# GpSimd's queue in source order, and single sums placed behind the last h product

## The chip, the cores and the metric

The kernel runs on one core of a Trainium2 chip. The metric is the device time of one execution in microseconds (us). Of a kernel there are several executions, and their median is given; one more view, the profile, comes from a single execution that was recorded instruction by instruction.

The engines of the core each have a queue of their own: TensorE (PE, matrix products and their weight loads), VectorE (DVE), ScalarE (ACT), GpSimd (POOL) and SyncE (SP). In this kernel GpSimd and SyncE issue transfers and compute nearly nothing.

## The reference

```python
def _attn_ref(q, k, v):                      # [8, 8, 576, 64] each, float32
    scores = scale * np.matmul(q, k.transpose(0, 1, 3, 2))
...
    mask = (rel >= 0) & (rel < 128)
    scores = np.where(mask, scores + bias[None], -1000000000.0)
...
    return np.matmul(attn, v)

def _moe_ref(x, w_gate, w_val, w_out):       # [4608, 512], [512, 1536] twice, [1536, 512]
    g = x @ w_gate
    silu = g * (1.0 / (1.0 + np.exp(-g)))
    return (silu * (x @ w_val)) @ w_out
```

Causal attention over a window of 128 positions with a linear bias per head; the heads side by side are x, 4608 tokens by 512, and x goes through a gated feed-forward. Inputs and output are float32 in DRAM; the kernel converts to fp16 as it loads.

## The kernel before, in words

**Attention.** The work is 36 units: four groups of two batches, nine tiles of 128 positions in each, of which the ninth holds the last 64 positions of both batches. A unit forms scores (products at L282 and L317), exponentials (ScalarE, L288 and L321), the multiplication by the mask and bias (L294), the product with V (L349), the division (L351, L352), and turns x for the second part.

**Loads.** For each tile (called its rank) there are three transfers on GpSimd's queue: k and q (`load_qk`, L191) into a pool of five buffers each, and V (`load_v`, L185) into one of twelve slots. `load` puts them in order for one rank. The queue of ranks 0 to 10 with the weights is written out by hand; from rank 11 on `attention()` calls `loads_to(i + 7)` after unit i. k and q have to be turned. Up to rank 10 TensorE does that (L215, L222); from rank 11 on a transposing transfer on SyncE's queue (L243) takes the buffer and writes kT (twelve slots) or qT (nine). A buffer of the pool comes free when its transposition has been done. From unit 24 on x is turned by such a transfer too (L370). The stores of the output (L447) go through SyncE as well.

**Feed-forward.** Nine blocks of 512 tokens, driven by the generator `ffn()`. Blocks 0 to 5 form gate and value plainly (L401) and give h = silu(gate) x value by L420 and L431, or, for the last four of twelve column blocks of block 5, by L428. Blocks 6 to 8 form them with seven products where eight would be plain (`gate_val_by_seven`, products at L627; VectorE's part at L663, L664, L670 and L679; the products `first` to `seventh` are named in the code). The output product of blocks 1 to 8 is done with seven products as well (`strassen`, L536, results by L540 and L551).

**Single sums.** Products with seven in place of eight need sums of their operands. They are formed on VectorE by short instructions of 128 x 512 in fp16: of h (`sums`, L489 to L492), of x (`x_sums`, the same lines) and of the gate and value weights (`gate_val_weight_sums`, L601 to L604, 24 in all, kept in memory that attention no longer needs). Most of them wait in a list, `later`, and `ffn()` takes one or two from it after each step (L725 in the plain blocks, L770 in the blocks by seven).

**The order.** Instructions of an engine run in the order of its queue. For the first tiles and the first steps the order on TensorE, VectorE and ScalarE is that of the source (`everything()`). After that a planner of the compiler's library orders them by its own estimates; from step 60 of `ffn()` on TensorE alone is held to the order of the source. GpSimd's and SyncE's queues and VectorE's and ScalarE's later part are the planner's.

Of the kernel before, what the change touches and what calls it, by code (L numbers as in the profile page):

```python
# [23 lines left out]
ET = mybir.EngineType  # L24
# [27 lines left out]
def kernel(  # L52
# [10 lines left out]
    nc = tc.nc  # L63
# [118 lines left out]
    def load_v(rank):  # L182
        va[rank] = va_all[rank % NV]
        for (p0, p1), src in source(v, rank):
            nc.gpsimd.dma_start(va[rank][p0:p1, :, 0:D], src)  # L185

    def load_qk(rank, which="kq"):
        for name in which:
            t_ = nat.tile([P, H, D], FP16, name=name + "n", tag=name + "n")
            for (p0, p1), src in source(k if name == "k" else q, rank):  # L190
                nc.gpsimd.dma_start(t_[p0:p1], src)  # L191
            (natk if name == "k" else natq)[rank] = t_

    def load(rank):
        if rank < 10:
            load_qk(rank)
            load_v(rank)
        else:
            load_v(rank)
            load_qk(rank)  # L200

    def transposed(name, rank):

# [184 lines left out]
    hT = {}  # L388
# [19 lines left out]
    acted = {}  # L408
# [14 lines left out]
    def val(n, m, pv, c0=0, c1=512):  # L423

        if n not in hT:
            hT[n] = hpool.tile([P, NMB, 512], FP16, name="hT", tag="hT")
        if (n, m) in by_silu:
            nc.vector.scalar_tensor_tensor(out=hT[n][:, m, c0:c1], in0=acted[(n, m)][0][:, c0:c1], scalar=2.0,  # L428
                                           in1=pv[:, c0:c1], op0=ALU.mult, op1=ALU.mult)
            return  # L430
        nc.vector.tensor_mul(hT[n][:, m, c0:c1], acted[(n, m)][1][:, c0:c1], pv[:, c0:c1])  # L431

    def gate_val(n, m):
        c0 = 384 if (n, m) in acted else 0
# [175 lines left out]
        s2, s3, s4 = xsum[n] = spare[3 * (n % 2):3 * (n % 2) + 3]  # L610
        return four_sums(a11, a12, a21, a22, s2, s3, s4)

    later = []

    def gate_val_by_seven(n):

        x = xT[n]
        A11, A12 = x[:, 0:HK, 0:256], x[:, HK:NKB, 0:256]
        S1, A22 = x[:, 0:HK, 256:512], x[:, HK:NKB, 256:512]
        S2, S3, S4 = xsum.pop(n)  # L620
        hT[n] = hpool.tile([P, NMB, 512], FP16, name="hT", tag="hT")
        live = {}

        def product(dst, w, c0, a, start=False):
            for i in range(2):
                for kb in range(HK):
                    nc.tensor.matmul(dst[:, i, :], w[:, kb, c0 + i * P:c0 + (i + 1) * P], a[:, kb, :],  # L627
                                     start=(start and i == 0 and kb == 0),
                                     stop=(i == 1 and kb == HK - 1), skip_group_check=True)

        def first(u):
            X, Y = (ps_a.tile([P, 2, 256], FP32, name=i, tag="a", bufs=4) for i in ("gX", "gY"))
            Z = ps_f.tile([P, 2, 256], FP32, name="gZ", tag="gv")
            live[u] = X, Y, Z
            product(X, G1, 2 * u * P, A11, True)
            nc.scalar.copy(Z, X)

        def fifth(u):
            Y = live[u][1]
            product(Y, tsum[u][0], 0, S1, True)  # L640
            p5 = epool.tile([P, 2, 256], FP32, name="p5", tag="exc", bufs=5)
            nc.scalar.copy(p5, Y)
            live[u] += (p5,)

        def second(u):
            Z = live[u][2]
            product(Z, G2, 2 * u * P, A12)
            s = supool.tile([P, 2, 256], FP16, name="s1", tag="tt")
            nc.scalar.activation(s, Z, AF.Silu)
            live[u] += (s,)  # L650

        def sixth(u):
            X = live[u][0]
            product(X, tsum[u][1], 0, S2)
            u2 = epool.tile([P, 2, 256], FP32, name="u2", tag="exc", bufs=5)
            nc.scalar.copy(u2, X)
            live[u] += (u2,)

        def third(u):
            X, Y, Z, p5, u2, s = live[u][:6]  # L660
            product(Y, V2, 2 * u * P, S4)
            v_ = supool.tile([P, 2, 256], FP16, name="v1", tag="uu")
            nc.vector.tensor_add(v_, Y, u2)  # L663
            nc.vector.tensor_mul(hT[n][:, 2 * u:2 * u + 2, 0:256], s, v_)  # L664

        def seventh(u):
            X, Y, Z, p5, u2, s = live[u]
            product(X, tsum[u][2], 0, S3)
            v_ = supool.tile([P, 2, 256], FP16, name="v2", tag="uu")
            nc.vector.tensor_add(v_, X, p5)  # L670
            live[u] += (v_,)

        def fourth(u):
            X, v_ = live[u][0], live[u][-1]
            del live[u]
            product(X, tsum[u][3], 0, A22)
            s = supool.tile([P, 2, 256], FP16, name="s2", tag="tt")
            nc.scalar.activation(s, X, AF.Silu)  # L678
            nc.vector.tensor_mul(hT[n][:, 2 * u:2 * u + 2, 256:512], s, v_)  # L679

        return {f.__name__: f for f in (first, second, third, fourth, fifth, sixth, seventh)}

    def seven_steps():
# [21 lines left out]
    def ffn():  # L705

        for n in range(NBLK):
            if n > 1:
                parts = chain(strassen(n - 1, 0), strassen(n - 1, 1))
            if n == 1:  # L710
                for j in range(PRE):
                    for _ in project(0, j, ps_f, "po", 1):
                        yield 1.0
            if n == SEVEN_FROM:
                break
            for m in range(NMB):
                for half, _ in enumerate(gate_val(n, m)):
                    yield 1.0
                    if n > 1 and 2 * m + half in AT:
                        next(parts)  # L720
                        yield 0.75
                    if n > 1:
                        for _ in range(1 + (len(later) > 3)):
                            if later:
                                later.pop(0)()  # L725
                if n == 1:
                    if m in (4, 6, 8, 10):
                        for _ in project(0, m // 2 - 2, ps_f, "po", 1):
                            yield 1.0
                    if m in (4, 6, 8):  # L730
                        weight_sums(m // 2 - 2)
                if n > 0 and m >= 9:
                    (at_once if n == 1 and m < 11 else later.extend)(sums(n, m - 9))
                if n + 1 == SEVEN_FROM:
                    if m == SILU_AT:
                        attention_ends()
                        by_silu.update((n, i) for i in range(m + 1, NMB))
                    if m in (SILU_AT + 1, SILU_AT + 2):
                        later.extend(gate_val_weight_sums(m - SILU_AT - 1))
                    if m == SILU_AT:  # L740
                        later.extend(x_sums(n + 1))
            if n > 1:
                assert next(parts, 0) == 0
        ends = [strassen(NBLK - 1, t) for t in range(2)]
        final = ()
        for n, k, name, which in seven_steps():
            if k == 0 and n > SEVEN_FROM:
                assert next(parts, 0) == 0
                parts = chain(strassen(n - 1, 0), strassen(n - 1, 1))
            if n == SEVEN_FROM and k in (1, 3, 10, 17):  # L750
                later.extend(gate_val_weight_sums(2 + (k + 4) // 7))
            yield 0.5
            if k % 3 == 1 and k < 42:
                next(parts)
                yield 0.75
            if k == 20 and n + 1 < NBLK:
                later.extend(x_sums(n + 1))
            if k == 35:
                later.extend(sums(n, 0))
            if name == "fourth" and which is not None and which[1] > 3:  # L760
                if which == (NBLK - 1, 5):
                    at_once(final)
                else:
                    later.extend(sums(which[0], which[1] - 3))
            if n == NBLK - 1 and k == 40:
                final = sums(n, 2)
                later.append(final.pop(0))
            for _ in range(2 if len(later) > 4 or k >= 39 or k < 7 else 1):
                if later:
                    later.pop(0)()  # L770
            if n == NBLK - 1 and k == 41:
                next(ends[0])
                yield 0.75
        assert next(parts, 0) == 0 and not later

        for t in (1, 0, 1, 0, 0, 0, 1, 0, 0, 1, 1, 1, 1):
            next(ends[t])
            yield 0.75
# [98 lines left out]
            nc.gpsimd.dma_start(dst[:, :, c0:c1], src[:, :, c0:c1])  # L877


    load_qk(1, "qk")  # L880
    load_qk(2, "q")
    load_v(0)
# [90 lines left out]
        held.close()  # L973

    everything()


# [28 lines left out]
```

## Time and profile before

| | us |
|---|---|
| median of 4 executions | 347.33 |
| lowest, highest | 346.94, 349.64 |
| the profiled execution | 349.64 |
| its span in the profile | 347.8 |
| TensorE busy in it | 331.7 |
| VectorE busy | 276.7 |
| ScalarE busy | 207.6 |
| GpSimd busy | 109.7 |

The span runs from the first to the last recorded instruction; the execution's own time is 1.84 us longer. A line of the waits names the engine that stood idle, the instruction that it stood at, and what ended the wait. In a timeline a line gives the start, the duration, the engine, the line of the kernel, the operation, and output <- inputs by the names of the program; a name such as kT at L601 to L604 is then the memory that the weight sum reuses. All line numbers are those of the kernel before.

### The profile page before, as it was taken

To read this page: it belongs to the slowest core of one execution; us is meant where nothing else is said; L and a number is where in the kernel's file an instruction comes from. 1 tells how busy PE (TensorE), PEld (TensorE's weight loads), DVE (VectorE), ACT (ScalarE), POOL (GpSimd) and SP (SyncE) were. 2 spreads that over 40 slices of the span, in tenths; PEclk is the share of its full clock that TensorE was granted. 3 is DMA by queue.
4 is the path that set the end of the run, shared out by engine and by line. 5 is a ranking of instruction groups with operands and counts; after the bars stand their busy time and mean duration, and the time that the engine had idled before them with its cause. 6 is when DMAs were issued, how large, how long until landed. Compare 5 with 4: busy or idle time off the path is not lost.

```text
span 347.8 us, 7788 instructions
## 1 busy us (share of the span) xinstructions
PE 331.7 (95%) x2983; PEld 219.3 (63%) x2983; DVE 276.7 (80%) x652; ACT 207.6 (60%) x412; POOL 109.7 (32%) x136
## 2 busy tenths in 40 slices
PE   7999987999999999999999999999999999999995
PEld 3584444344446655556556565566688878878884
DVE  5477884799978869988899999999855875775583
ACT  3758674465667557575575556563467666766750
POOL 8977585258537654735511000000000000000000
PEclk9999998999999999999999999999999999999999
DMA  9999999999999999999999203021101101011014
GB/s 151 171 180 174 153 160 170 106 125 144 152 149 136 183 159 140 184 133 165 138 158 183 89 21 92 15 57 52 62 0 62 62 0 63 1 62 60 2 62 122
DMA packets 160037, 37.37 MB, mean 107 GB/s; under 512 B 147328, under 2 KB 155648, under 8 KB 160000
## 3 DMA queue, kind: packets, MB, share of 16 engines
q0 software_dynamic: 118336, 18.62, 84.6%
q1 hardware_dynamic: 40976, 17.64, 28.5%
q10 hardware_dynamic: 688, 0.62, 0.6%
q8 instruction: 23, 0.38, 0.5%
q14 instruction: 14, 0.11, 0.1%
HBM read 37.91 MB, written 9.44 MB: 136 GB/s over the span
## 4 chain that ended last, share of the span: by engine, by line
PE 63%; DVE 21%; ACT 6%; DMA 5%; issue 3%; POOL 0%; SPq 0%; DVEq 0%; ACTq 0%
PE po L536 13%; PE pg L401 12%; PE pv L401 12%; PE gX L627 6%; PE av L349 3%; DMA wo_sb<-in_moe_w_out_dram 3%; DVE hT L431 3%; PE gY L627 3%; DVE uu L420 3%; PE ps L282 3%; PE p L536 2%; PE po L455 2%; ACT ex L288 2%; DVE S L489 2%; DVE hT L490 2%
## 5 line engine op out<-in xcount | busy, mean ns | idle before, releaser
L401 PE MATMUL pv<-xT,wv_sb 128*128 128x512 f16 (+2 forms) x320 | 76.5, 358 | 0.4 <-DVE hT L431 0.2
L401 PE MATMUL pg<-xT,wg_sb 128*128 128x512 f16 (+2 forms) x320 | 76.0, 359 | 0.3 <-DVE xT L377 0.2
L419 ACT ACTIVATE tt<-pg 128x512 f16<-128x512 f32 (+2 forms) x70 | 41.3, 590 | 50.5 <-PE pg L401 49.5
L288 ACT ACTIVATE ex<-ps 128x512 f16<-128x512 f32 x96 | 50.0, 606 | 12.0 <-PE ps L282 11.9
L420 DVE SCALAR_TENSOR_TENSOR uu<-tt,pg 128x512 f16<-128x512 f16 (+2 forms) x69 | 45.8, 664 | 10.5 <-ACT tt L419 10.2
L431 DVE TENSOR_TENSOR hT<-uu,pv 128x512 f16<-128x512 f16 (+2 forms) x70 | 46.5, 665 | 3.6 <-PE pv L401 1.6
L191 POOL DMA_DIRECT2D kn<-in_k_dram x39 | 33.1, 852 | 34.8 <-DMA kT<-kn 24.7
L401 PEld LDWEIGHTS <-wg_sb 128*128 128x128 f16 x320 | 28.3, 98 | 24.6 <-issue 2.7
L401 PEld LDWEIGHTS <-wv_sb 128*128 128x128 f16 x320 | 28.3, 98 | 23.7 <-issue 2.6
L536 PEld LDWEIGHTS <-hT 128*128 128x128 f16 x384 | 36.8, 98 | 10.0 <-issue 1.1
L185 POOL DMA_DIRECT2D va<-in_v_dram x40 | 34.1, 857 | 19.8 <-PE av L349 8.4
L191 POOL DMA_DIRECT2D qn<-in_q_dram x39 | 33.1, 852 | 16.4 <-DMA qT<-qn 6.6
L536 PEld LDWEIGHTS <-S 128*128 128x128 f16 x288 | 27.6, 98 | 11.9 <-DVE S L491 2.5
L294 DVE TENSOR_TENSOR ex<-ex,m_reg 128x1024 f16<-128x1024 f16 x42 | 28.6, 685 | 3.2 <-ACT ex L288 3.1
L352 DVE TENSOR_TENSOR x<-av,rec 128x256 f16<-128x256 f32 x72 | 28.5, 418 | 0.4
L536 PE MATMUL po<-T,S 128*128 128x256 f16 x192 | 26.7, 273 | 1.5 <-DVE S L491 1.5
L536 PE MATMUL po<-T,hT 128*128 128x256 f16 x192 | 26.1, 273 | 0.0
L679 DVE TENSOR_TENSOR hT<-s,v 128x512 f16<-128x512 f16 x18 | 7.6, 423 | 21.4 <-ACT s L678 21.4
L321 ACT ACTIVATE exc<-psc 128x512 f16<-128x512 f32 x40 | 21.3, 608 | 4.1 <-PE psc L317 4.1
L349 PEld LDWEIGHTS <-ex 128*128 128x128 f16 x384 | 17.4, 97 | 4.6 <-issue 1.3
L349 PE MATMUL av<-va,ex 128*128 128x65 f16 x384 | 19.3, 193 | 0.7 <-ACT ex L288 0.7
L379 ACT COPY xT<-px 128x512 f16<-128x512 f16 x20 | 11.7, 584 | 8.9 <-PE px L375 8.7
(134 smaller groups left out, 543.1 us busy)
## 6 DMA issues: line engine op xcount, KB each, us to landing
out_dram<-osb SPq DMA_DIRECT2D x32, 256.0 KB, 3.3
va<-in_v_dram POOLq DMA_DIRECT2D x32, 128.0 KB, 8.3
qn<-in_q_dram POOLq DMA_DIRECT2D x31, 128.0 KB, 8.1
kn<-in_k_dram POOLq DMA_DIRECT2D x31, 128.0 KB, 8.2
wg_sb<-in_moe_w_gate_dram POOLq DMA_DIRECT2D x6, 256.0 KB, 8.1
wv_sb<-in_moe_w_val_dram POOLq DMA_DIRECT2D x6, 256.0 KB, 8.0
wo_sb<-in_moe_w_out_dram POOLq DMA_DIRECT2D x2, 768.0 KB, 9.8
kn<-in_k_dram POOLq DMA_DIRECT2D x8, 64.0 KB, 9.4
```

Source lines behind the costliest of these rows:

```text
L185: nc.gpsimd.dma_start(va[rank][p0:p1, :, 0:D], src)
L191: nc.gpsimd.dma_start(t_[p0:p1], src)
L288: nc.scalar.activation(e[:, o:o + 2, :], banks[q4][par], AF.Exp, scale=scale)
L294: nc.vector.tensor_mul(e[:, o, :], e[:, o, :], reg[:, o, :])
L349: nc.tensor.matmul(av[:, j, :], w, val, start=(n == 0), stop=(n == len(todo) - 1))
L352: nc.vector.tensor_mul(x[:, 4 * half:4 * half + 4, :], av[:, :, 0:D], rec.broadcast_to([P, 4, D]))
L401: nc.tensor.matmul(ps[:, c0:c1], w[:, kb, ms], xT[n][:, kb, c0:c1], start=(kb == 0 and c0 == 0), stop=(kb == NKB - 1 and c1 == 512), skip_ ...
L419: nc.scalar.activation(tt, pg[:, c0:c1], AF.Tanh, scale=0.5)
L420: nc.vector.scalar_tensor_tensor(out=uu, in0=tt, scalar=one if (n, m) == PIN else 1.0, in1=pg[:, c0:c1], op0=ALU.add, op1=ALU.mult)
L431: nc.vector.tensor_mul(hT[n][:, m, c0:c1], acted[(n, m)][1][:, c0:c1], pv[:, c0:c1])
L536: nc.tensor.matmul(dst, a[:, m, cols], b[:, m, :], start=(start and m == 0), stop=(m == HM - 1), skip_group_check=True)
L627: nc.tensor.matmul(dst[:, i, :], w[:, kb, c0 + i * P:c0 + (i + 1) * P], a[:, kb, :], start=(start and i == 0 and kb == 0), stop=(i == 1 an ...
```

## The change

There are three edits. `load` no longer distinguishes ranks: k and q are issued ahead of V for every rank (the earlier form put V first from rank 10 on). The whole queue of GpSimd is held to the order of the source. And a single sum that is taken from `later` is put on VectorE's queue behind the h product that the source wrote last (`anchor`); this is an order on the same queue and adds no semaphore. The h products by L428 are not recorded as anchors.

```diff
     def load(rank):
-        if rank < 10:
-            load_qk(rank)
-            load_v(rank)
-        else:
-            load_v(rank)
-            load_qk(rank)
+        load_qk(rank)
+        load_v(rank)
...
-        nc.vector.tensor_mul(hT[n][:, m, c0:c1], acted[(n, m)][1][:, c0:c1], pv[:, c0:c1])
+        anchor[0] = nc.vector.tensor_mul(hT[n][:, m, c0:c1], acted[(n, m)][1][:, c0:c1], pv[:, c0:c1]).ins
...
-    later = []
+    later, anchor = [], [None]
+
+    def one_later():
+
+        with tc.issue_after(anchor[0]):
+            later.pop(0)()
...
-            nc.vector.tensor_mul(hT[n][:, 2 * u:2 * u + 2, 0:256], s, v_)
+            anchor[0] = nc.vector.tensor_mul(hT[n][:, 2 * u:2 * u + 2, 0:256], s, v_).ins
...
-            nc.vector.tensor_mul(hT[n][:, 2 * u:2 * u + 2, 256:512], s, v_)
+            anchor[0] = nc.vector.tensor_mul(hT[n][:, 2 * u:2 * u + 2, 256:512], s, v_).ins
...
                             if later:
-                                later.pop(0)()
+                                one_later()
...
                 if later:
-                    later.pop(0)()
+                    one_later()
...
+    queue = ExitStack()
+    queue.enter_context(tc.manual_schedule(engines={ET.Pool}))
     load_qk(1, "qk")
...
     everything()
+    queue.close()
```

## The prediction

> **What bounds the kernel now.** I read the page first (busy times, the 40 slices), then the waits of TensorE, then the busy time of each engine by stretches of 10 us, and last the timeline around the waits that lie where the change acts.
>
> ```profile
> PE 331.7 (95%) x2983; PEld 219.3 (63%) x2983; DVE 276.7 (80%) x652; ACT 207.6 (60%) x412; POOL 109.7 (32%) x136
> ```
>
> TensorE is the bound: 347.8 - 331.7 = 16.1 us of the span is idle on it, and start and end (about 2.4 and 3.8 us) and the stretch from 20 to 60 us (about 4.3 us) hold most of that. Whatever the change does can only shorten or lengthen waits of TensorE. Who they wait for:
>
> ```profile
> PE po L455 <- DMA wo_sb<-in_moe_w_out_dram: 2.1, 1, 2.1
> PE po L536 <- DVE S L491: 1.5, 3, 0.6
> PE po L536 <- DVE osb L540: 1.5, 2, 0.8
> ...
> PE gX L627 <- DVE v L670: 0.6, 3, 0.2
> ...
> PE pt L222 <- DMA qn<-in_q_dram: 0.4, 1, 0.4
> ```
>
> (Total us, times, longest.) The first is a weight load at 57 us, which the change does not move. No product waits for a transposed k or q, and the one load of q that is waited for is at 28 us. The rows with VectorE, together 3.6 us, are what a new order on VectorE can give back or add to. VectorE is full in one stretch and loose in the next:
>
> ```profile
> 180.00:190.00 10.00, 10.00 (x94) 5.87 (x91) 10.00 (x26) 6.62 (x14) 0.89 (x1) 1.00 1.60 209
> 190.00:200.00 10.00, 9.16 (x80) 5.52 (x79) 9.41 (x24) 5.10 (x10) 0.00 (x0) 1.00 0.32 90
> 220.00:230.00 10.00, 9.34 (x95) 5.47 (x93) 10.00 (x27) 5.16 (x11) 0.00 (x0) 1.00 0.13 26
> 260.00:270.00 10.00, 10.00 (x94) 8.96 (x92) 5.13 (x10) 7.16 (x15) 0.00 (x0) 1.00 0.15 54
> ```
>
> (After the length: PE, weight load, VectorE, ScalarE, GpSimd.) From 170 to 250 us VectorE is at 9.4 to 10 of 10; from 250 on at 5 to 8.7.
>
> **What the Trainium skill says.** "Perfetto Trace Analysis", Per-engine timelines: VectorE, ScalarE and GpSimd execute strictly in order. The trace agrees: at 60.68 us GpSimd issued a load, and then nothing for 6.58 us, because the next load in its queue waited. So an order imposed on these queues is what runs. "DMA: Bandwidth & Descriptors", Issuing engines are not separate DMA queues: transfers of all issuers share the same 16 DMA engines. The trace agrees: 128 KB loads land about 0.9 us apart at the start, but 1.6 to 1.78 us apart from 71 to 118 us, where transposing transfers from SP run beside them. "VectorE: DVE Perf Modes", the perf-mode tier table: a PSUM operand costs tensor_tensor its faster mode. Here a 512-wide fp16 sum takes 415 ns (next start about 335 ns later) and L670, which reads PSUM, 687 ns (about 600 ns later). These intervals are my prices.
>
> **The change, part by part.** The order of instructions on TensorE and on ScalarE is the same in both kernels; only GpSimd (and SP with it) and VectorE run in another order, with the same instructions.
>
> (1) *GpSimd's queue.* In it the planner had put Q12 and V12 to V16 ahead of K12's load, which waits for the transposition of K11 out of its buffer:
>
> ```profile
> 60.68 0.88 POOL L185 DMA_DIRECT2D va<-in_v_dram  x1 [0.50 <-issue]
> 68.14 1.75 POOL L191 DMA_DIRECT2D kn<-in_k_dram  x2 [6.58 <-DMA kT<-kn]
> ```
>
> In source order everything behind K12 waits with it: k, q, V of 12, then of 13, and so on. K11's transposition landed at 67.6 us; with fewer loads ahead it comes a little sooner, K12 lands at about 69.5, and one load follows each 1.6 us. A transposition takes 7 to 8 us from issue. Q12 is then in place at about 78, and unit 11 takes it at 82.1. Q14 (7 loads after K12) lands at 69.5 + 7 x 1.6 = 80.7, and must by 84; Q17 (16 loads) at 95.1, and must by 101. The margins are 3 to 6 us and then grow, as a tile takes three loads, 4.8 us, and a unit some 6.2 us. V24 and V33 wait for their slot until 126 and 183 us; K34 and K35 behind the latter land by 200 and are used from 215. On SP the stores and the transpositions of x stand behind those of k and q, which come later: eight output buffers and x not wanted before some 210 us cover that. At the start V0 goes ahead of K2: one load, 0.9 us, against 2.4 us between K2's landing (10.8) and its use (13.25). I cost the whole part at 0; the cover is those 3.3 us at Q14. Gone, it costs what Q14 to Q17 are late. A gain is excluded: no wait of TensorE after 28 us has a k, q or V load behind it.
>
> (2) *Single sums tied on VectorE.* Up to now the planner put them anywhere after their operands. Now each stands behind the h product that the source last wrote (L431, L664 or L679). I laid the new order over the trace, each instruction with its measured interval, started no earlier than its operands' times; what moves is this.
>
> - Five weight sums (L601 to L604) at 181.3, 186.8, 187.7, 188.1 and 189.0 leave the queue ahead of L540:
>
> ```profile
> 189.02 0.41 DVE L601 TENSOR_TENSOR qT<-wv_sb,wg_sb 128x512 f16<-128x512 f16 x1
> ...
> 192.62 0.42 DVE L540 SCALAR_TENSOR_TENSOR osb<-po,p5s 128x256 f32<-128x256 f32 x1
> ```
>
>  5 x 0.335 = 1.68 us earlier, more than TensorE's wait of 0.84 us for it at 193.09; the neighbours' own operands leave 0.08: -0.76.
> - At 222 to 223 L491 comes 0.15 earlier, but a mask multiply L294 (0.60) gets ahead of L540: -0.15 + 0.53 = +0.38.
> - The weight sums reappear in the first units of block 6 (255 to 265 us), ahead of L670 there, which comes 0.63, 0.78 and 0.65 later. Most is slack before the fourth product: +0.05, +0.20, +0.32 = +0.57.
> - Two short waits for L670 at 279 and 307 shrink: -0.13 each, -0.26.
> - The sums of the last h products of blocks 6 and 7, for which L536 waits:
>
> ```profile
> 309.58 0.42 DVE L490 TENSOR_TENSOR hT<-hT 128x512 f16<-128x512 f16 x1
> 309.91 0.68 DVE L663 TENSOR_TENSOR v<-gY,u 128x512 f16<-128x512 f32 x1
> 310.51 0.41 DVE L491 TENSOR_TENSOR S<-hT 128x512 f16<-128x512 f16 x1
> 310.85 0.42 DVE L664 TENSOR_TENSOR hT<-s,v 128x512 f16<-128x512 f16 x1
> 310.99 0.39 PE L536 MATMUL po<-T,S 128*128 128x256 f16 x2 [0.35 <-DVE S L491]
> ```
>
>  L489 now comes first here and L491 goes behind L664: two more instructions ahead of it, 2 x 0.335 = +0.66. At 282.6 the same two, less 0.3 from sums of x that no longer hold up L679: +0.39.
> - At the end (331 to 337): +0.10.
>
> In block 5 the h products by L428 are not recorded, so what comes there stays tied to the last L431, earlier in the queue: no added delay. What is queued behind a tied sum is only VectorE's next work, which is counted above; the tie is no wait of its own. Sum: -0.76 + 0.38 + 0.57 - 0.26 + 0.39 + 0.66 + 0.10 = +1.08 us. The profiled execution took 349.64 us, 1.84 more than its span: span 347.8 + 1.1 = 348.9, time 350.7. That run lies 2.3 us above the median of the four, so on the median: 347.33 + 1.08 = **348.4 us**. Both ends: if the delays of L670 in block 6 count in full (2.06 for 0.57) and at 282.6 the sums of x give nothing back, 1.08 + 1.49 + 0.3 = +2.9, 350.2. If no later wait grows, the next rival.
>
> **Rivals.**
>
> *Slower by the load queue.* K12's wait holds Q12 to Q17 back. For it: the 6.6 us of waiting, which the planner had filled beforehand with five loads, and a GpSimd that needs 0.85 us to issue each load and so catches up no faster than the transfers. Against: the margins above. It decides where a load takes more than about 2.07 us (84 = 69.5 + 7 x 2.07). Loads and transpositions are denser here than the trace of before shows anywhere, so 2.3 us is possible: Q14 lands at 85.6, Q17 at 106.3, 5.3 late, and with the other part's 1 us TensorE ends at about 353; at 2.15 us about 351.5.
>
> *Faster by relief of VectorE.* 24 weight sums, 24 x 0.335 = 8 us, leave the stretch where VectorE has no gap for one where it has 15 to 50%. If the waits at 193, 222 and 223 go (0.84 + 0.51 + 0.15) and those at 279 and 307 shrink, while the later sums stay hidden, it is -1.8 to -2.1: 345.3. All waits for VectorE after 60 us with their refill are about 5 us, so 342 is the floor. Against: the sums for L536 at 282 and 311 are already the last thing to be ready, and the new order puts more ahead of them.
>
> *Nothing that can be told.* TensorE's order is untouched, and the sums are so short that slack takes both sides: within 0.5 us, 347.3.
>
> **How the numbers follow.** Forecast (347.6 to 350) 0.55; load queue 0.14; relief 0.14; nothing 0.17. The likeliest gives 348.4. The range leaves the lower half of relief and the upper half of the load queue outside: 345.3 to 351.8. A difference under 1% (3.5 us: below 343.9, above 350.8) is about what a measurement of this kernel cannot tell from none. Faster by that would take nearly all of VectorE's waits: 0.04. Slower: the load queue and the upper edge of the forecast: 0.16. Within: 0.80.
>
> **What would show it.** Right: the wait of L536 for L491 goes from 1.5 to about 2.5 us in total, that for L540 from 1.5 to about 1.1; L601 to L604 stand from 240 us on; VectorE below 10 of 10 from 180 to 200 and above 5.5 from 255 to 270; GpSimd idle from about 53 to 66 us and no product (L282, L317) that waits for kT or qT. Wrong: a TensorE wait for a transposition between 80 and 120 us (load queue), or L491's waits not above before's (relief). A forecast this small also fails if refill after a wait costs more than the visible gap.

## The result, and the profile after

The changed kernel takes 349.44 us (median of 43 executions) where the kernel before takes 347.29 (64). The ratio is 1.0058, 95% interval 1.0044 to 1.0072: it is slower by 2.0 us, 1.5 to 2.5. The prediction was +1.08 us on the median, inside a range of 347.6 to 350.

The profiled execution of the changed kernel has a span of 347.4 us, 0.4 less than the one of before. That comparison misleads, because the profiled execution of before had a lapse of the TensorE clock: it was granted half the clock from 57.7 to 61.1 us and lost about 1.5 us there, long before the change moves anything on VectorE. A second profile of the same kernel without such a lapse has a span of 345.7 us (below). On record, the mean granted clock of an execution is either 0.992 to 0.995 or 0.997 and more; 3.4 us at half clock in a span of 347.8 give 0.995, so the first group is called "with a lapse" below, though the lapse itself was only seen in profiles. Of the changed kernel 12 of 44 recorded executions belong to it, and their median is 2.4 us above that of the others.

TensorE runs the same 2983 products in the same order in all kernels here, so they can be set against each other one by one: at each product, its start in one kernel less its start in the other. Where this difference steps up, time was lost, and where it steps down, time was won.

The busy times of the changed kernel and its waits of TensorE (total us, times, longest; `wo_sb` holds the output weights, `osb` is a buffer of results). Line numbers have moved: L532 is L536 of before, L536 is L540, L487 is L491, L671 is L670, L664 and L665 are L663 and L664, L680 is L679, L597 to L600 are L601 to L604.

```profile
PE 330.6 (95%) x2983; PEld 218.4 (63%) x2983; DVE 277.9 (80%) x652; ACT 207.8 (60%) x412; POOL 109.6 (32%) x136
```

```profile
PE po L532 <- DVE S L487: 2.4, 3, 1.0
PE po L451 <- DMA wo_sb<-in_moe_w_out_dram: 1.9, 1, 1.9
...
PE gX L628 <- DVE v L671: 1.0, 4, 0.3
...
PE po L532 <- DVE osb L536: 0.6, 1, 0.6
```

The busy times have not moved. The wait of the output product for S, the sums of h, has grown from 1.5 to 2.4 us, that for L671 (L670 before) from 0.6 to 1.0, and that for osb has shrunk from 1.5 to 0.6. VectorE's load, by stretches of 10 us (PE, weight load, VectorE, ScalarE, GpSimd busy):

```profile
180.00:190.00 10.00, 10.00 (x93) 6.02 (x90) 9.76 (x24) 5.15 (x11) 7.60 (x10) 1.00 1.76 85
190.00:200.00 10.00, 10.00 (x94) 6.13 (x92) 8.21 (x20) 5.14 (x11) 0.00 (x0) 1.00 1.24 155
220.00:230.00 10.00, 9.59 (x100) 5.92 (x100) 8.70 (x22) 5.74 (x12) 0.00 (x0) 1.00 0.11 22
260.00:270.00 10.00, 9.71 (x90) 8.55 (x89) 7.31 (x17) 7.01 (x14) 0.00 (x0) 1.00 0.08 28
```

VectorE has air from 180 to 200 us now and again from 220 to 230 (from 210 to 220 it is still full), and from 260 to 270 it is at 7.3 where it was at 5.1: the weight sums have moved. TensorE is without a gap from 190 to 200 (9.16 before) and has one at 260.

The end of block 7, the place shown before the change:

```profile
308.25 0.41 DVE L485 TENSOR_TENSOR S<-hT 128x512 f16<-128x512 f16 x1
308.59 0.68 DVE L664 TENSOR_TENSOR v<-gY,u 128x512 f16<-128x512 f32 x1
...
309.19 0.41 DVE L486 TENSOR_TENSOR hT<-hT 128x512 f16<-128x512 f16 x1
309.52 0.41 DVE L665 TENSOR_TENSOR hT<-s,v 128x512 f16<-128x512 f16 x1
309.86 0.41 DVE L487 TENSOR_TENSOR S<-hT 128x512 f16<-128x512 f16 x1
...
310.33 0.39 PE L532 MATMUL po<-T,S 128*128 128x256 f16 x2 [1.01 <-DVE S L487]
```

The sum at L485 and the h product at L665 now stand ahead of the sum that TensorE waits for, and the wait is 1.01 where it was 0.35. On GpSimd:

```profile
51.13 0.90 POOL L185 DMA_DIRECT2D va<-in_v_dram  x1
62.82 0.88 POOL L191 DMA_DIRECT2D kn<-in_k_dram  x1 [10.79 <-DMA kT<-kn]
```

The load of K12 waits 10.8 us, but it is issued at 62.8, 5.3 us sooner than before, as the transposition of K11 landed sooner (62.3 instead of 67.6). No product waits for k, q or V afterwards.

Where the difference to the kernel before steps, in us, with the places named by their time in the profile shown of before (0 stands for less than 0.02). "From 173 us" is the change of the difference from 173 us (behind the last wait for a V load) to the end. The columns of the runs belong to the experiments below.

| place | predicted | changed kernel | weight sums tied | h and x tied | last h sums tied | sums first |
|---|---|---|---|---|---|---|
| 193, L540 | -0.76 | -0.85 | -0.85 | -0.14 | 0 | -0.84 |
| 210, L540 | 0 | 0 | 0 | 0 | 0 | +0.33 |
| 222 and 223 | +0.38 | +0.42 | 0 | +0.47 | 0 | +0.22 |
| 245, L540 | 0 | +0.25 | 0 | 0 | 0 | +0.59 |
| 255 to 265, mostly L670 | +0.57 | +0.78 | +0.45 | 0 | 0 | 0 |
| 279 and 307, L670 | -0.26 | +0.18 | 0 | +0.40 | -0.23 | 0 |
| 282, L491 | +0.39 | +0.37 | 0 | +0.37 | +0.67 | -0.47 |
| 311, L491 | +0.66 | +0.67 | 0 | +0.67 | +0.77 | -0.47 |
| 312 to 338 | +0.10 | +0.11 | 0 | +0.11 | 0 | 0 |
| from 173 us | +1.08 | +1.92 | -0.37 | +1.90 | +1.25 | -0.62 |

### The profile page after: what moved, and what is told of

The parts are those of the page before. It is cut to its first block, busy times and chain, and to the rows that moved or that the text cites. A ratio compares the mean times of both kernels' runs of the same rounds, so it can differ in the third digit from the quotient of the medians.

```text
span 347.4 us, 7775 instructions
## 1 busy us (share of the span) xinstructions
PE 330.6 (95%) x2983; PEld 218.4 (63%) x2983; DVE 277.9 (80%) x652; ACT 207.8 (60%) x412; POOL 109.6 (32%) x136
## 4 chain that ended last, share of the span: by engine, by line
PE 65%; DVE 16%; DMA 7%; ACT 6%; issue 2%; POOL 1%; ACTq 0%; DVEq 0%; POOLq 0%
PE po L532 14%; PE pv L397 13%; PE pg L397 13%; PE gX L628 6%; PE av L345 4%; DMA wo_sb<-in_moe_w_out_dram 3%; PE ps L278 3%; PE gY L628 3%; PE p L532 3%; DMA va<-in_v_dram 3%; PE po L451 2%; DVE hT L427 2%; ACT tt L415 1%; DVE v L671 1%; PE gZ L628 1%
## 5 line engine op out<-in xcount | busy, mean ns | idle before, releaser
L532 PEld LDWEIGHTS <-hT 128*128 128x128 f16 x384 | 36.8, 98 | 10.1 <-issue 1.1
L532 PEld LDWEIGHTS <-S 128*128 128x128 f16 x288 | 27.5, 98 | 12.3 <-DVE S L487 3.4
L532 PE MATMUL po<-T,S 128*128 128x256 f16 x192 | 26.7, 273 | 2.4 <-DVE S L487 2.4
L532 PE MATMUL po<-T,hT 128*128 128x256 f16 x192 | 26.0, 273 | 0.0
L317 ACT ACTIVATE exc<-psc 128x512 f16<-128x512 f32 x40 | 21.4, 607 | 4.2 <-PE psc L313 4.1
L680 DVE TENSOR_TENSOR hT<-s,v 128x512 f16<-128x512 f16 x18 | 7.6, 424 | 18.1 <-ACT s L679 18.0
L278 PE MATMUL ps<-qT,kT 64*128 64x256 f16 x192 | 16.5, 272 | 0.4 <-DVE qT L223 0.2
```

What stands on the lines that cost most here:

```text
L532: nc.tensor.matmul(dst, a[:, m, cols], b[:, m, :], start=(start and m == 0), stop=(m == HM - 1), skip_group_check=True)
```

## The experiments

The theory: all of the loss comes from VectorE's order, and most of it from two sums at the ends of blocks 6 and 7, each with two more instructions ahead of it. The rivals: the load queue (late k, q or V), the weight sums, or many small delays spread over all sums. The traces have the same order on TensorE and on ScalarE in every kernel. Times are set against the kernel before on the same chip. Their intervals are some 0.2% wide on either side, so it is the steps in the traces that separate effects of half a microsecond.

**The load queue alone.**

```diff
     def one_later():
-        with tc.issue_after(anchor[0]):
-            later.pop(0)()
+        later.pop(0)()
```
(against the changed kernel)

> GpSimd's queue in source order with k, q, V per rank, and no ties: TensorE, ScalarE and VectorE run in the order of the kernel before, GpSimd in that of the changed one. Theory (all of the loss comes from VectorE's order): 0 within 0.4 us of the kernel before, and no product that waits for kT or qT. Rival (late loads or transpositions cost it): +1 to +2 us, with waits between 60 and 130 us or on V.

Ratio 1.002 (0.9993 to 1.0046). VectorE's order is that of the kernel before, and no product waits for k, q or V after 60 us. From 61 us to the end the difference to the kernel before changes from 0.65 to 0.49 us ahead; 0.10 of that is one step at 311 us, where L551 starts 0.43 us behind L679 and not 0.34, and why it does is not shown. So the load queue costs 0.1 us or so at most, and the rival falls. The median is higher because of lapses of the clock (6 of 14 executions, against 6 of 51 of before): without them the mean is 347.34 against 347.24. The kernel was profiled once more, together with the kernel before:

> GpSimd's queue in source order without ties once more, for a second profile. Theory: no wait of L349 for V at any clock; waits on wo_sb (L455) of 1 to 2 us. From 61 us on the same TensorE times as the kernel before but for that wait.

Span 346.1; a wait for wo_sb of 2.0, none for V; 0.10 ahead of the second profile of before at 57 us and 0.01 at the end, with the same step of 0.10 at 311. As expected.

> The kernel before once more, for a second profile. If the granted clock stays at 0.997 or more, the stretch from 57 to 61 us is some 1.5 us shorter than in the profile shown, and L349 then waits about 1 us for a V load near 110 us, as in the three runs that have the planner's GpSimd queue and a full clock. If the clock is lower again, neither. Rival: no wait for V in either case, and it belongs to the ties.

Span 345.7 at a mean clock of 0.998. The time from 57 to 61 us is shorter by 1.5 us, as expected, but L349 waits for V only once, for 0.3 us, and at 167 us, not at 110; what this costs is regained at 172. So a full clock alone does not bring the wait at 110 us. The wait for wo_sb was 1.9 us in this execution, and TensorE came to the V at 110 us after it had landed.

**The ties alone**, with GpSimd's queue and `load` as before.

> The ties alone; GpSimd's queue is the planner's as before, VectorE's order is that of the changed kernel. Theory: the whole loss, +1.7 to +2.1 us; L536's waits for L491 at the ends of blocks 6 and 7 (about 1.0 us each) as in the changed kernel. Rival (load queue): under +1 us.

Ratio 1.0068 (1.0041 to 1.0095), +2.4 us, and +1.97 from 173 us on, step for step as in the changed kernel; VectorE runs the same order in both. The whole loss is in the ties. Beside that a wait showed that the changed kernel doesn't have:

```profile
PE po L536 <- DVE S L491: 2.4, 3, 1.0
PE av L349 <- DMA va<-in_v_dram: 1.3, 1, 1.3
...
PE po L455 <- DMA wo_sb<-in_moe_w_out_dram: 0.5, 1, 0.5
```

wo_sb came early here and TensorE was 1.58 us ahead of the second profile of before at 57 us. At 110 us it lost 1.42 us to a V load. In the four runs that waited for it, all with the planner's queue, the product with that V started between 110.0 and 110.8 us.

**The weight sums alone tied**, and the rest alone.

```diff
     def one_later():
-        with tc.issue_after(anchor[0]):
-            later.pop(0)()
+        f = later.pop(0)
+        if f in weights:
+            with tc.issue_after(anchor[0]):
+                f()
+        else:
+            f()
```
(`weights` collects what `gate_val_weight_sums` returns; the other run has `f not in weights`; both with GpSimd's queue as before)

> Only the 24 weight sums are tied; sums of h and x stay the planner's. Theory: the wait of 0.84 us at 193 us goes, and about 1.0 us comes back at 245 to 265 us in block 6: +0.2 us within 0.5. Rival (the weight sums are the cause): +1.5 or more. Rival (relief of VectorE): -0.7 or less.

Ratio 1.0011 (0.9992 to 1.0031). In the trace -0.85 at 193 and +0.45 in block 6, -0.37 from 173 us on: a small gain where +0.2 was expected, because without the tied sums of x and h beside them the weight sums cost nothing at 245 and less in block 6. Neither rival holds.

> Only the sums of h and x are tied; the weight sums stay the planner's, between 181 and 250 us. Theory: the wait at 193 us stays, L536 waits about 1.0 us each at the ends of blocks 6 and 7, and some 0.4 near 222 us: +1.6 us within 0.5. Rival (the weight sums are the cause): under +0.6.

Ratio 1.0065 (1.0046 to 1.0084), +2.3 us, and +1.90 from 173 us on. The ties of h and x are the cause.

**Which of them.** Only the eight sums of the last h products (u = 5) of blocks 6 and 7 tied, then all of h and x but those.

```diff
-                    later.extend(sums(which[0], which[1] - 3))
+                    h_sums = sums(which[0], which[1] - 3)
+                    if which[1] == 5:
+                        last_sums.update(h_sums)
+                    later.extend(h_sums)
```
(`one_later` ties `f in last_sums`; in the other run `f not in last_sums and f not in weights`)

> Of all sums only the eight of the last h products of blocks 6 and 7 (u = 5) are tied; all else is the kernel before. Theory (two instructions more ahead of L491 at each of these two places): L536 waits about 1.0 us for L491 at each, 0.45 and 0.7 us more than before, +1.2 us within 0.4. Rival (it is the many other sums, spread): under +0.4.

Ratio 1.0022 (1.0002 to 1.0042), +0.8 us, and in the trace +1.25 from 173 us on. VectorE's order is that of before until 275 us. The end of block 6 in the kernel before:

```profile
281.22 0.41 DVE L490 TENSOR_TENSOR hT<-hT 128x512 f16<-128x512 f16 x1
...
281.55 0.68 DVE L663 TENSOR_TENSOR v<-gY,u 128x512 f16<-128x512 f32 x1
...
282.15 0.41 DVE L491 TENSOR_TENSOR S<-hT 128x512 f16<-128x512 f16 x1
282.49 0.42 DVE L664 TENSOR_TENSOR hT<-s,v 128x512 f16<-128x512 f16 x1
...
282.62 0.39 PE L536 MATMUL po<-T,S 128*128 128x256 f16 x2 [0.65 <-DVE S L491]
```

And in this run:

```profile
279.46 0.42 DVE L489 TENSOR_TENSOR S<-hT 128x512 f16<-128x512 f16 x1
...
279.80 0.68 DVE L672 TENSOR_TENSOR v<-gY,u 128x512 f16<-128x512 f32 x1
280.40 0.42 DVE L490 TENSOR_TENSOR hT<-hT 128x512 f16<-128x512 f16 x1
280.73 0.42 DVE L673 TENSOR_TENSOR hT<-s,v 128x512 f16<-128x512 f16 x1
281.06 0.42 DVE L491 TENSOR_TENSOR S<-hT 128x512 f16<-128x512 f16 x1
...
281.54 0.39 PE L536 MATMUL po<-T,S 128*128 128x256 f16 x2 [1.32 <-DVE S L491]
```

Eight tied instructions out of some hundred put L489 and L664 (L673 here; L672 is L663) ahead of L491, and the wait of 0.65 becomes 1.32. In the changed kernel the same two stand ahead of it.

> All sums of h and x are tied but those eight; the weight sums are the planner's. Theory: the waits at the ends of blocks 6 and 7 are those of the kernel before (0.65 and 0.35), and only the half microsecond near 222 us and some tenths in block 7 stay: +0.5 us within 0.5. Rival (spread over all sums): +1.5.

Ratio 0.9989 (0.9973 to 1.0005), +0.36 from 173 us on by the trace; the times show no loss. So the eight carry about two thirds of the 1.90, the others 0.36; the missing 0.3 comes only when both are tied, at 307 us, where the wait for L670 grows by 0.31 (-0.12 with the eight alone, +0.09 with the others alone). At 282 the two parts add up: +0.67 with the eight, -0.30 with the others, +0.37 with both.

**Can the gain be had without the loss?** The weight sums may start from about 198 us, behind an h product of block 4, and the others are the planner's.

```diff
+        if (n, m) == (4, 6):
+            early_h[0] = anchor[0]
...
+        if f in weights:
+            with tc.issue_after(early_h[0]):
+                f()
+        else:
+            f()
```
(against the changed kernel)

> GpSimd's queue as in the changed kernel, sums of h and x the planner's, and the weight sums tied behind one h product of block 4 (m = 6), so that they may start from about 198 us and none stands ahead of L540 at 192. Theory: the wait of 0.84 at 193 us goes as in the changed kernel, and block 6 loses nothing as the sums are done by 245 us: -0.8 us within 0.5. Rival (a full VectorE only moves its wait to the next place, 222 us): 0.

Ratio 1.0005 (0.9983 to 1.0027). The 0.84 at 193 are won, but at 210, 222 to 223 and 245 it loses 0.33, 0.22 and 0.59: the rival held. Eight microseconds of sums moved within a full stretch delay the next L540 instead of this one.

The other way at L491: L663, which holds VectorE for 0.60 us, is put behind it.

```diff
-            nc.vector.tensor_add(v_, Y, u2)
+            if u == 0 and n > SEVEN_FROM:
+                with tc.issue_after(s2_last[0]):
+                    nc.vector.tensor_add(v_, Y, u2)
+            else:
+                nc.vector.tensor_add(v_, Y, u2)
```
(on top of the last; `s2_last` is the L491 of the last h product of the block before)

> As the run with the weight sums behind block 4, and in blocks 7 and 8 the first L663 is put behind L491 of the last h product of the block before, so that L491 has one instruction of 0.60 less ahead of it. Theory: the waits of L536 at the ends of blocks 6 and 7 (0.65 and 0.35) shrink to under 0.1: -1.7 us against the kernel before, within 0.5. Rival (L663 is late then and TensorE waits for it or its PSUM bank instead): -0.8 or worse.

Ratio 0.9953 (0.9934 to 0.9972): 1.6 us faster than the kernel before. In the trace TensorE gains 0.47 at the end of block 6 and 0.47 at that of block 7, and nothing else comes late for it; what the previous run lost stays lost. The end of block 6 (L488, L489 and L675 are L490, L491 and L663 of before):

```profile
278.33 0.42 DVE L488 TENSOR_TENSOR hT<-hT 128x512 f16<-128x512 f16 x1
...
278.78 0.43 DVE L489 TENSOR_TENSOR S<-hT 128x512 f16<-128x512 f16 x1
279.12 0.68 DVE L675 TENSOR_TENSOR v<-gY,u 128x512 f16<-128x512 f32 x1
...
279.26 0.39 PE L534 MATMUL po<-T,S 128*128 128x256 f16 x2 [0.18 <-DVE S L489]
```

The gain is 0.47 and not the 0.60 of L663, because L491 now follows L490, whose result it reads, and starts 0.45 us behind it (278.33 to 278.78). The instruction that follows next and does not read the result of the one before starts after 0.34 (278.78 to 279.12). In the kernel before the same holds throughout: where L491 follows L490 at once, it starts 0.45 to 0.46 us behind it, six times out of six. The predicted price of 0.335 us thus holds for neighbours that don't need each other.

The trace explains only part of the 1.6 us: from 173 us on this kernel wins 0.62. Where the rest comes from is not shown. Its profiled execution was 1.0 us ahead of the second profile of before at 61 us already, where VectorE's order is that of before; but so was that of the previous run (1.1), whose median gained nothing. Lapses of the clock are not all of it: 1 of 22 executions has one here, 15 of 67 of before, and without them the means still differ by 1.3 us.

**The best of each**: the weight sums tied as in the changed kernel, the sums of h and x the planner's, and L663 behind L491, once with GpSimd's queue in source order and once with the planner's.

```diff
-            with tc.issue_after(early_h[0]):
+            with tc.issue_after(anchor[0]):
```
(against the run before; the second run also has `load` and GpSimd's queue of the kernel before)

> Source-order queue; weight sums tied behind the last h product as in the changed kernel; sums of h and x the planner's; the first L663 of blocks 7 and 8 behind L491. Theory from the traces: -0.8 at 193, +0.4 near 260, -0.47 and -0.46 at the ends of blocks 6 and 7, so -1.3 us from 61 us on, where the run with the weights behind block 4 had -0.6; about 345.5 us. Rival (what the weight sums cost in block 6 comes on top, as L663 is late there): no better than 346.1.

Ratio 0.999 (0.9969 to 1.0011) with a median of 346.45; the profiled execution has a span of 343.0 us, the shortest of all, and 1.6 us of its lead on the second profile of before stand already at 57 us, as wo_sb landed early. With the queue in source order it kept this lead at 110 us. From 173 us on it wins 1.36, as expected. The expected time of 345.5 was not reached in the median.

> The same VectorE order with the planner's GpSimd queue and V ahead of k and q from rank 10. Theory: L349 waits about 1.2 us for V near 110 us, TensorE having been 0.5 us earlier at 61 us: +0.3 to +1.0 us against the run with the source-order queue. Rival (the queue makes no difference): within 0.3.

Ratio 0.9979 (0.996 to 0.9998), median 347.02; -1.36 from 173 us on. L349 did not wait for V, so the expected wait was not put to the test: wo_sb was late in this execution (a wait of 1.9 us) and TensorE not early. The two runs don't differ beyond their intervals, and the queue's order is worth nothing that these runs can tell.

By the trace both should gain twice what the run before them gained, and by their medians they don't. Lapses of the clock hide it: 4 of 12 and 10 of 22 executions have one, against 3 of 33 of the kernel before. Without them the means are 345.88 and 345.85 against 347.16 of before, gains of 1.28 and 1.31, near the 1.36 of both traces. Whether these kernels are more prone to lapses, or happened to be run when there were many, is not shown. The same sorting gives +1.84 for the ties alone, +1.99 for h and x, -0.33 for the weight sums and +0.99 for the eight, near the traces. It does less well for h and x without the eight (-0.13, where the trace has +0.36), and the run with L663 behind L491 keeps its 0.7 us that the trace lacks.

## Why the prediction was right, and where its sizes were off

*GpSimd's queue at 0.* Right, to 0.1 us. It is shown by the run with the queue alone and by its repetition. The margins were larger than worked out: K12 was not issued at some 66 to 68 us but at 62.8, because "a little sooner" for K11's transposition was 5 us (it landed at 62.3 and not at 67.6). Q14's transposition was issued at 77.2 and Q17's at 90.8 us, where the prediction had them landing at 80.7 and 95.1. From K12 (66.4) to Q17, 16 loads, the transpositions were issued (90.8 - 66.4)/16 = 1.53 us apart, as the loads landed, near the 1.6 taken and far from the 2.07 at which it would have decided.

*-0.76 at 193.* Right: -0.85, and shown by the weight sums alone.

*+0.38 at 222.* Right: +0.42 (-0.18 and +0.60), with a mask multiply ahead of L540 as forecast.

*+1.05 at the ends of blocks 6 and 7.* Right: +0.37 and +0.67, and the mechanism, more instructions ahead of L491, was isolated by tying eight sums (+1.25 from 173 us on) and turned round by moving L663 behind it (-0.94). The two terms of the 0.39 at 282 came out one by one: two more instructions cost 0.67 with the eight sums tied, and the others gave 0.30 back.

*+0.57 in block 6.* The right place, at +0.78. The first two delays were rated at 0.05 and 0.20 and measured 0.10 and 0.24, the third at 0.32 and 0.44.

*0 at 245.* Wrong, by 0.25. The prediction priced the weight sums only where they come back "in the first units of block 6 (255 to 265 us)", though it names 240 us among its signs. Those of the first two column pairs come back at once, from 239 us on, in the last stretch of block 5, where VectorE is still full:

```profile
240.30 0.41 DVE L600 TENSOR_TENSOR kT<-wg_sb,kT 128x512 f16<-128x512 f16 x1
240.64 0.42 DVE L597 TENSOR_TENSOR kT<-wv_sb,wg_sb 128x512 f16<-128x512 f16 x1
240.97 0.42 DVE L598 TENSOR_TENSOR kT<-wv_sb 128x512 f16<-128x512 f16 x1
...
241.31 0.42 DVE L599 TENSOR_TENSOR kT<-wv_sb,kT 128x512 f16<-128x512 f16 x1
241.65 0.42 DVE L597 TENSOR_TENSOR kT<-wv_sb,wg_sb 128x512 f16<-128x512 f16 x1
...
242.58 0.41 DVE L536 SCALAR_TENSOR_TENSOR osb<-po,p5s 128x256 f32<-128x256 f32 x1
```

The L540 that the output product waits for (L536 here) stands behind them. It takes the ties of x and h as well: with the weight sums alone tied, they come back as early and nothing is lost at 245.

*-0.26 at 279 and 307.* Wrong in sign: +0.18. L670 comes a little later there, not earlier. With the eight last sums alone tied the forecast came true (-0.11 and -0.12). With the sums before them tied too, one more, the L489 that the planner had done ahead of L679, stands between L679 and L670.

So the sum of 1.08 was short by 0.84, and 0.69 of that lies in the last two terms (0.25 and 0.44). The measured +2.0 agrees with the trace's +1.92 from 173 us on, within its interval. That it lies within the range owes something to luck: the upper end allowed for delays of L670 in block 6 and for sums of x at 282, and these gave 0.2 more and nothing more than the forecast, while the larger misses came at places that were rated at nothing or as a gain. The rivals fell: relief of VectorE was real (-0.85) but with the weight sums alone tied 0.37 of it remain, as the same instructions are late elsewhere; the load queue stayed hidden; and it was not nothing.

The expected signs mostly came: the wait for L491 2.4 (2.5 forecast), the weight sums from 239 us, VectorE at 9.76 and 8.21 of 10 from 180 to 200, GpSimd idle from 52 to 62.8. The wait for L540 fell to 0.6 where 1.1 was forecast, since the new loss at 222 is booked on the products of L317, whose wait for L540 grew from 0.2 to 0.8, and not on L536.

## What to carry to other kernels

Put the new order of a non-bounding engine against the waits of the bounding one place by place. A tie "behind X" cost time here where it put instructions ahead of one that a product was waiting for, and there it cost about the intervals of those instructions; at the other places it cost nothing that the traces show. Eight instructions made about two thirds of this loss, 1.25 us, and moving one longer instruction behind the awaited one won 0.94. Price an instruction by the interval to the next start, and look whether the next one reads its result: for the sums of 128 x 512 here it was 0.34 us if not, 0.45 if so. And where the order on the bounding engine is unchanged, compare two traces product by product, not span by span: a difference in the first 61 us hid a loss of 2 us here. Sort the executions by their granted clock too, before their medians are compared: two kernels that gained 1.3 us without lapses gained 0.9 and 0.4 by their medians.

## What the runs showed that was not expected

The profiled executions differ by up to 3.8 us at 61 us, before anything that these kernels change on VectorE. Two things make this up. The wait for wo_sb was between none and 2.6 us. And in three profiles TensorE was granted half the clock for 3.4 us, beginning between 56.5 and 57.7 us, which cost about 1.5 us. These three had waits for wo_sb of 2.1, 2.2 and 2.6 us; the profiles with waits of 2.0 us or less had no lapse, and one with 2.1 had none either. So the two seem to go together, but what sets a lapse off is not shown. From 50 to 61 us alone the profiles differ by up to 4.0 us, more than the ties cost.

An early start is not always kept. In three runs with the planner's queue TensorE came to a V load at 110 us early, and lost 1.3 to 1.5 us there each time; three runs with the source-order queue were 1.0 to 1.6 us ahead and lost nothing. The three that lost also have the sums of h and x tied, which changes VectorE's order from 87 us on, so the queue alone is not shown to be the cause. The ties are not needed for such a wait: the run with the eight sums tied, in VectorE's order of before up to 275 us and no earlier at 110 us than the second profile of before, lost 0.57 there too, as that V landed later.
